# One reciprocal of eight columns in place of two of four, for the two head groups of a q tile

## Chip, cores and metric

The kernel runs on one core of one Trainium2 chip. The metric is the device time of one execution, in microseconds (us); several runs are taken and their median is quoted. The profile is of one further execution, recorded instruction by instruction.

## What is computed

Random-feature attention, followed by two feed-forward blocks, all in float32:

```
phi(x) = exp(x @ omega.T - |x|^2/2 - max) / sqrt(M)
kv  = einsum('bhsm,bhsd->bhmd', phi(k), v)
z   = sum over s of phi(k)
num = einsum('bhsm,bhmd->bhsd', phi(q), kv)
den = einsum('bhsm,bhm->bhs', phi(q), z) + 1e-06
x   = num / den                        # 4 batches x 8 heads x 576 x 64
x   = softplus(x @ w_in) @ w_out       # 2304 tokens, 512 -> 2048 -> 512
out = ((x @ w1) * (x @ w2)) @ w3 @ w_out2
```

## The kernel before

The 2304 tokens are 18 tiles of 128. A first stage makes `kv` for each batch and group of four heads, with `z` as a 65th column beside the 64 of `v` (a column of ones is appended to `v`). A second stage, the **q stage** (the loop at L767, from about 55 to 133 us of the span), turns the 18 q tiles into `x`. Then come the large products of the feed-forward blocks, from about 123 us to the end; they take some 680 of the 811 us.

In the q stage a tile is worked on in two **units**, one for each group of four heads. For a unit, in the order of the dataflow:

- `q_feat` (L393, with `project` at L339): twelve matmuls into one PSUM bank; `nmax`, the row maximum, by VectorE (L349, DVE in the profile); then four exponentials by ScalarE (L354, ACT) into `qp`.
- `q_turn` (L406): transposes of `qp` by TensorE (L409, PE) into a PSUM bank and one copy out by ACT (L411) into `qpt`.
- `q_num` (L413): the matmuls of `qpt` with `kv` (L96, recorded as `ps<-kv,qpt`) into a bank of their own, 65 columns for each head: 64 of the numerator and one of the denominator. Then three operations of DVE, each on four heads: L426 adds a small constant to the four denominators and writes them to a small tile `den`, L427 takes the reciprocal of these four columns in place, and L430 multiplies the 256 numerators by them and writes half of `xt`. L430 is the last reader of the bank.

After both units, `x_turn` (L435) transposes the tile's `xt` on PE (L439), ACT or DVE copies the result out (L444 or L442), and a DMA of the SP queue writes it to a DRAM tensor `xd`. When six tiles are there, `operands` (L448) reads them back for the first feed-forward product.

The stages are shifted against each other: in step t of the loop the features of tile t, the transposes of tile t-2, the numerators of tile t-3 and the `x_turn` of tile t-4 are issued. In odd steps `numerators` (L762) runs at the start and in even steps at the end, so that two tiles, four units, follow each other on PE with no other work between them. There are eight such pairs and two single tiles at the ends. The splitting of the weights and of the operands for the next stage is put into the same loop from a list, at fixed rates for each step.

All products of the kernel share eight PSUM banks (`ps`, L81), taken in turn. A new product waits until the last reader of the bank is done. The order of each engine's instructions is fixed when the program is built: a scheduler takes instructions in the order of the code but lets a later one pass an earlier one that it estimates is not ready yet. So DVE's order in the trace mixes units, and puts other work between two steps of a unit. Each engine runs its list strictly in that order.

The denominators of two consecutive units already lie in one tile of 2 x 4 columns (`pair`, L274, with three buffers).

Of the kernel before, what the change touches and what calls it, by code (L numbers as in the profile page):

```python
# [19 lines left out]
F32 = mybir.dt.float32  # L20
# [4 lines left out]
ALU = mybir.AluOpType  # L25
AX = mybir.AxisListType

B, H, S, D = 4, 8, 576, 64
M = 128
NT = B * S  # L30
# [41 lines left out]
def body(ctx: ExitStack, tc: tile.TileContext, q, k, k_rest, v, v_rest, om_t, w_in, w_out, w12, w3, wo, out):  # L72
    nc = tc.nc
    cp = ctx.enter_context(tc.tile_pool(name="cp", bufs=1))
    sm = ctx.enter_context(tc.tile_pool(name="sm", bufs=1))
    M_ = ctx.enter_context(tc.tile_pool(name="M_", bufs=14))
# [6 lines left out]
    def ps():  # L83
        return ps_.tile([128, 512], F32, tag="ps", name="ps")
# [10 lines left out]
    def matmul(o, a, b, start, stop, **kw):  # L95
        nc.tensor.matmul(out=o, lhsT=a, rhs=b, start=start, stop=stop, **kw)  # L96
# [177 lines left out]
    def pair(name, bufs):  # L274
        n = small.get(name, (None, 1))[1]
        if n:
            small[name] = sm.tile([128, 2, 4], F32, tag=name, bufs=bufs, name=name), 0
        else:
            small[name] = small[name][0], 1
        return small[name][0][:, 1 - bool(n)]  # L280
# [9 lines left out]
    kt, vt, kps, kpr, kvs, qts, kacc, raw = {}, {}, {}, {}, {}, {}, {}, {}  # L290
# [84 lines left out]
    def matmul_half(o, a, b, start, stop):  # L375
        for c in range(0, a.shape[-1], HALF):
            matmul(o[c:c + HALF], a[:, c:c + HALF], b, start, stop, skip_group_check=True)
# [11 lines left out]
        nc.scalar.copy(out=kvs[b][:, 4 * g:4 * g + 4, :], in_=acc)  # L389

    qp, qpt, xt = {}, {}, {}

    def q_feat(u):  # L393
        t, g = divmod(u, 2)
        p = project(lambda p: [x[:, 2 * g + p, :] for x in qts[t]])
        if g and t >= NT // 128 - len(EARLY):
            free["X0"] += 2

        def exps():
            qp[u] = M_.tile([128, 4, M], F32, tag="m", name="qp")  # L400
            features(*p, qp[u])

        waiting.append(exps)
        flush(QLAG)
# [5 lines left out]
        qpt[u] = M_.tile([128, 4, 128], F32, tag="m", name="qpt")  # L410
        nc.scalar.copy(out=qpt[u], in_=tp.rearrange("p (h t) -> p h t", h=4))  # L411

    def q_num(u):  # L413
        t, g = divmod(u, 2)
        nm = ps()
        nm = nm[:, 0:4 * (D + 1)].rearrange("p (h d) -> p h d", h=4)
        lo, hi = 128 * t, 128 * t + 128
        for h in range(4):
            a = lo
            while a < hi:  # L420
                b = a // S
                e = min(hi, (b + 1) * S)
                matmul_half(nm[a - lo:e - lo, h, :], qpt[u][:, h, a - lo:e - lo], kvs[b][:, 4 * g + h, :], True, True)
                a = e
        den = pair("den", 3)[:, :, None]
        nc.vector.tensor_scalar(out=den, in0=nm[:, :, D:D + 1], scalar1=1e-6 * M, scalar2=None, op0=ALU.add)  # L426
        nc.vector.reciprocal(out=den, in_=den)  # L427
        if g == 0:
            xt[t] = M_.tile([128, H, D], F32, tag="m", name="xt")
        nc.vector.tensor_tensor(  # L430
            out=xt[t][:, 4 * g:4 * g + 4, :], in0=nm[:, :, 0:D],
            in1=den.to_broadcast([128, 4, D]), op=ALU.mult,
        )

    def x_turn(t):  # L435
        tp = ps()
# [314 lines left out]
    nt = NT // 128  # L751
    begun = None

    def fill():
# [3 lines left out]
            x = Up1(0, 0, UP_RATES["Up1"][0])  # L758
            begun = x, x.begin_parts()
        next(begun[1], None)  # L760

    def numerators(t):  # L762
        if 0 <= t < nt:
            for g in range(2):
                q_num(2 * t + g)

    for t in range(nt + XLAG):  # L767
        if t % 2:
            numerators(t - NLAG)
        for g in range(2):  # L770
            if 0 <= t - TLAG < nt:
                q_turn(2 * (t - TLAG) + g)
        for g in range(2):
            if t < nt:
                q_feat(2 * t + g)
            else:
                flush(0)
            step(JOB_Q[0 in xo])
        for x in [nt - len(EARLY) + n for n, at in enumerate(EARLY) if at == t] + [t + 2] * (t + 2 < nt - len(EARLY)):
            split_q(x)  # L780
            load_q()
        if t == 1:
            kv_sum(2 * B - 1)
            kstack.close()
            pools["X0"] = ctx.enter_context(tc.tile_pool(name="X0", bufs=28, side="right", reuse_waits="tile"))
        if t >= XLAG:
            x_turn(t - XLAG)
            for c in range(2):
                if t - XLAG == 2 * N // 128 * (c + 1) - 1:
                    xo[c], ops = operands(c, xd, "X0")  # L790
                    queue += ops
        if not t % 2:
            numerators(t - NLAG)
        if t in FILL:
            fill()
# [426 lines left out]
```

## Time and profile before

| | us |
|---|---|
| median of 3 runs | 811.22 |
| lowest, highest | 810.95, 811.86 |
| profiled execution, its own time | 813.02 |
| profiled execution, span of its instructions | 810.9 |

The span is the time from the first to the last recorded instruction. An operation's duration in the trace is longer than the time for which it keeps its engine: the next one can start before the end of the one before. Where the cost of one more instruction is asked, the distance from its start to the next start is what counts. The ends of matmuls are modelled, so PE's busy share is not its use; the number of matmuls in a stretch tells more.

### The profile page before, as it was taken

The page shows a single profiled execution, that of the slowest core. Times are in us where ns is not written, and L with a number is a line of the kernel's source. Part 1 is how long each engine was busy: PE and PEld are TensorE (multiplying, and loading weights), DVE is VectorE, ACT ScalarE, POOL GpSimd, SP SyncE. Part 2 cuts the span into 40 slices and gives each one's busy share as a digit, 9 for nine tenths or more (in the row PEclk, how much of TensorE's full clock was granted, in tenths as well). Part 3 has the DMA queues.
Part 4 walks back from the last instruction along what each step waited for, and adds up shares of the span by engine and source line. Part 5 has one row for each costly group of instructions (what it writes and reads, how often), then busy time and mean ns, then how long its engine had stood idle before and what let it go on. Part 6 is the DMA issues. An engine that isn't in the chain of part 4 may idle for free.

```text
span 810.9 us, 14465 instructions
## 1 busy us (share of the span) xinstructions
PE 804.0 (99%) x5462; PEld 752.4 (93%) x5462; DVE 602.3 (74%) x1022; ACT 441.2 (54%) x859; POOL 26.5 (3%) x29
## 2 busy tenths in 40 slices
PE   9999999999999999999999999999999999999998
PEld 8999999999999998888888889999999998889998
DVE  6999999878765676754569633897988876888861
ACT  6999998557445676646456432424335123674330
POOL 3033300000000000000000000000000000000000
PEclk9999999999999999999999999999999999999999
DMA  9833635656535558688994642365656556353212
GB/s 288 327 100 87 201 107 172 210 205 214 195 133 195 191 193 259 214 258 293 335 304 148 208 127 79 133 217 186 209 174 214 188 180 237 111 170 122 73 65 78
DMA packets 75861, 150.04 MB, mean 185 GB/s; under 512 B 7184, under 2 KB 44688, under 8 KB 75792
## 3 DMA queue, kind: packets, MB, share of 16 engines
q1 hardware_dynamic: 64016, 101.55, 38.1%
q10 hardware_dynamic: 11776, 47.57, 17.4%
q8 instruction: 43, 0.70, 0.4%
q14 instruction: 26, 0.21, 0.1%
HBM read 98.24 MB, written 50.86 MB: 184 GB/s over the span
## 4 chain that ended last, share of the span: by engine, by line
PE 92%; DVE 4%; DMA 2%; issue 1%; ACT 0%; POOL 0%; ACTq 0%; POOLq 0%
PE ps L96 90%; DMA xq<-xd 1%; PE ps L409 1%; DVE nmax L349 1%; DVE xt L430 1%; DVE s L462 1%; PE ps L439 0%; DVE c L517 0%; DMA rawq<-in_q 0%; DVE u L517 0%; DVE xa22l L472 0%; DVE xa12l L472 0%; DVE qt L297 0%; DVE qtl L298 0%; DVE tlo L191 0%
## 5 line engine op out<-in xcount | busy, mean ns | idle before, releaser
L96 PE MATMUL ps<-dhi,lo 128*128 128x512 f32 x256 | 99.6, 389 | 0.0
L96 PE MATMUL ps<-dlo,hi 128*128 128x512 f32 x256 | 99.6, 389 | 0.0
L96 PE MATMUL ps<-dhi,hi 128*128 128x512 f32 x256 | 99.4, 389 | 0.0
L642 DVE TENSOR_TENSOR dlo<-dn,dhi 128x512 fp32r<-128x512 f32 x64 | 43.8, 689 | 39.1 <-ACT dhi L641 23.0
L517 DVE TENSOR_TENSOR c<-ps,u 128x384 f32<-128x384 f32 x144 | 71.5, 550 | 0.8
L517 DVE TENSOR_TENSOR u<-ps,p 128x384 f32<-128x384 f32 x48 | 26.7, 556 | 53.9 <-PE ps L96 52.3
L524 ACT COPY p<-ps 128x384 f32<-128x384 f32 x48 | 23.0, 480 | 75.8 <-PE ps L96 57.3
L641 ACT CAST dhi<-dn 128x512 fp32r<-128x512 f32 x64 | 39.4, 619 | 45.2 <-DVE dlo L642 25.7
L142 DVE SCALAR_TENSOR_TENSOR f<-raw,f 128x1024 int32<-128x1024 f32 (+2 forms) x43 | 45.5, 1058 | 20.3 <-ACT raw L139 18.8
L557 ACT ACTIVATE c<-c 128x384 f32<-128x384 f32 x72 | 35.1, 524 | 46.8 <-DVE c L517 43.0
L96 PEld LDWEIGHTS ps<-dlo,hi 128*128 128x128 f32 x256 | 48.1, 188 | 10.0
L96 PEld LDWEIGHTS ps<-dhi,hi 128*128 128x128 f32 x256 | 48.1, 188 | 10.0
L96 PEld LDWEIGHTS ps<-dhi,lo 128*128 128x128 f32 x256 | 48.1, 188 | 9.8
L138 ACT ACTIVATE f<-raw,bias 128x1024 f32<-128x1024 int16 (+2 forms) x43 | 46.3, 1084 | 18.9 <-DMA raw<-in_w 9.3
L349 DVE TENSOR_REDUCE nmax<-ps 128x4 f32<-128x512 f32 x72 | 47.0, 683 | 6.2 <-PE ps L96 6.0
L139 ACT ACTIVATE raw<-raw,bias 128x1024 f32<-128x1024 int16 (+2 forms) x43 | 46.3, 1082 | 0.6
L148 DVE SCALAR_TENSOR_TENSOR f<-raw,f 128x1024 int32<-128x1024 int32 (+2 forms) x43 | 45.0, 1046 | 0.6
L354 ACT ACTIVATE qp<-ps,nmax 128x128 f32<-128x128 f32 x144 | 42.2, 457 | 2.4 <-DVE nmax L349 2.4
L354 ACT ACTIVATE kp<-ps,nmax 128x128 f32<-128x128 f32 x128 | 35.5, 460 | 6.0 <-DVE nmax L349 5.9
L96 PE MATMUL ps<-xs1h,thi 128*128 128x384 f32 x96 | 32.4, 337 | 0.2 <-DVE c L517 0.2
L96 PE MATMUL ps<-xs2h,thi 128*128 128x384 f32 x96 | 32.3, 336 | 0.0
L96 PE MATMUL ps<-xs2h,tlo 128*128 128x384 f32 x96 | 32.2, 335 | 0.0
(257 smaller groups left out, 2339.4 us busy)
## 6 DMA issues: line engine op xcount, KB each, us to landing
dn<-gd SPq DMA_DIRECT2D x64, 256.0 KB, 4.0
raw<-in_w ACTq DMA_DIRECT2D x16, 1023.8 KB, 5.8
gd<-c SPq DMA_DIRECT2D x80, 192.0 KB, 2.7
pd<-c SPq DMA_DIRECT2D x48, 192.0 KB, 2.7
raw<-in_w_out ACTq DMA_DIRECT2D x10, 767.8 KB, 4.6
raw<-in_w_in ACTq DMA_DIRECT2D x6, 1023.8 KB, 5.1
rawq<-in_q SPq DMA_DIRECT2D x18, 256.0 KB, 3.1
xd<-xs SPq DMA_DIRECT2D x18, 256.0 KB, 3.3
```

What stands on the lines that cost most here:

```text
L96: nc.tensor.matmul(out=o, lhsT=a, rhs=b, start=start, stop=stop, **kw)
L138: nc.scalar.activation(out=self.f, in_=top, func=AF.Relu, scale=TOP, bias=bias[:, 0:1])
L139: nc.scalar.activation(out=self.words(1, F32, 2), in_=top, func=AF.Identity, scale=TOP, bias=bias[:, 1:2])
L142: nc.vector.scalar_tensor_tensor(out=self.f.bitcast(I32), in0=self.words(1, F32, 2), scalar=-2.0 ** 31, in1=self.f, op0=ALU.max, op1=ALU.min)
L148: nc.vector.scalar_tensor_tensor(out=fi, in0=self.words(0, I32, 2), scalar=13, in1=fi, op0=ALU.logical_shift_right, op1=ALU.bitwise_or,)
L349: nc.vector.tensor_reduce(out=nmax, in_=pj, axis=AX.X, op=ALU.max, negate=True)
L354: nc.scalar.activation(out=dst[:, h, :], in_=pj[:, h, :], func=AF.Exp, bias=nmax[:, h:h + 1])
L517: nc.vector.tensor_tensor(out=z, in0=bank, in1=y, op=ALU.add)
L524: nc.scalar.copy(out=p6, in_=b1)
L557: nc.scalar.activation(out=dst, in_=src, func=AF.Softplus)
L641: nc.scalar.copy(out=hi, in_=got[m])
L642: nc.vector.tensor_tensor(out=lo, in0=got.pop(m), in1=hi.bitcast(F32), op=ALU.subtract)
```

## The change

`q_num` for a unit and `numerators` for a tile become one function for a tile. It issues the matmuls of both units into two banks, then both additions into one tile `den` of 2 x 4 columns, then one reciprocal of the eight columns, then both multiplications. The matmuls, the additions and the multiplications are the same instructions as before, 36 of each of the two DVE operations; the reciprocals are 18 in place of 36. The `den` tile has the same size and number of buffers as before. The helper moves up in the file, and `nt` with it.

```diff
--- before.py
+++ after.py
@@ -389,6 +389,7 @@
         nc.scalar.copy(out=kvs[b][:, 4 * g:4 * g + 4, :], in_=acc)
 
     qp, qpt, xt = {}, {}, {}
+    nt = NT // 128
 
     def q_feat(u):
         t, g = divmod(u, 2)
@@ -410,27 +411,31 @@
         qpt[u] = M_.tile([128, 4, 128], F32, tag="m", name="qpt")
         nc.scalar.copy(out=qpt[u], in_=tp.rearrange("p (h t) -> p h t", h=4))
 
-    def q_num(u):
-        t, g = divmod(u, 2)
-        nm = ps()
-        nm = nm[:, 0:4 * (D + 1)].rearrange("p (h d) -> p h d", h=4)
+    def numerators(t):
+        if not 0 <= t < nt:
+            return
+        nms = []
         lo, hi = 128 * t, 128 * t + 128
-        for h in range(4):
-            a = lo
-            while a < hi:
-                b = a // S
-                e = min(hi, (b + 1) * S)
-                matmul_half(nm[a - lo:e - lo, h, :], qpt[u][:, h, a - lo:e - lo], kvs[b][:, 4 * g + h, :], True, True)
-                a = e
-        den = pair("den", 3)[:, :, None]
-        nc.vector.tensor_scalar(out=den, in0=nm[:, :, D:D + 1], scalar1=1e-6 * M, scalar2=None, op0=ALU.add)
+        for g in range(2):
+            nm = ps()[:, 0:4 * (D + 1)].rearrange("p (h d) -> p h d", h=4)
+            for h in range(4):
+                a = lo
+                while a < hi:
+                    b = a // S
+                    e = min(hi, (b + 1) * S)
+                    matmul_half(nm[a - lo:e - lo, h, :], qpt[2 * t + g][:, h, a - lo:e - lo], kvs[b][:, 4 * g + h, :], True, True)
+                    a = e
+            nms.append(nm)
+        den = sm.tile([128, 2, 4, 1], F32, tag="den", bufs=3, name="den")
+        for g in range(2):
+            nc.vector.tensor_scalar(out=den[:, g], in0=nms[g][:, :, D:D + 1], scalar1=1e-6 * M, scalar2=None, op0=ALU.add)
         nc.vector.reciprocal(out=den, in_=den)
-        if g == 0:
-            xt[t] = M_.tile([128, H, D], F32, tag="m", name="xt")
-        nc.vector.tensor_tensor(
-            out=xt[t][:, 4 * g:4 * g + 4, :], in0=nm[:, :, 0:D],
-            in1=den.to_broadcast([128, 4, D]), op=ALU.mult,
-        )
+        xt[t] = M_.tile([128, H, D], F32, tag="m", name="xt")
+        for g in range(2):
+            nc.vector.tensor_tensor(
+                out=xt[t][:, 4 * g:4 * g + 4, :], in0=nms[g][:, :, 0:D],
+                in1=den[:, g].to_broadcast([128, 4, D]), op=ALU.mult,
+            )
 
     def x_turn(t):
         tp = ps()
@@ -759,11 +764,6 @@
             begun = x, x.begin_parts()
         next(begun[1], None)
 
-    def numerators(t):
-        if 0 <= t < nt:
-            for g in range(2):
-                q_num(2 * t + g)
-
     for t in range(nt + XLAG):
         if t % 2:
             numerators(t - NLAG)
```

## Rows read from the trace of the kernel before

**Rows 1.** The page, part 1: busy time, share of the span and instructions of each engine.

```profile
PE 804.0 (99%) x5462; PEld 752.4 (93%) x5462; DVE 602.3 (74%) x1022; ACT 441.2 (54%) x859; POOL 26.5 (3%) x29
```

**Rows 2.** Stretches: length, busy us (x instructions) of PE, PEld, DVE, ACT, POOL, clock, DMA.

```profile
82.50:91.30 8.80, 8.02 (x113) 7.39 (x112) 8.74 (x24) 7.81 (x24) 3.29 (x3) 1.00 0.53 151
91.30:99.00 7.70, 7.70 (x116) 7.41 (x114) 7.02 (x20) 6.95 (x22) 3.06 (x3) 1.00 0.68 212
...
150.00:715.00 565.00, 565.00 (x2965) 524.73 (x2966) 401.24 (x648) 275.02 (x426) 0.00 (x0) 1.00 0.60 199
```

**Rows 3.** The waits of PE between 57 and 133 us: total, times, longest.

```profile
PE ps L409 <- ACT qp L354: 0.6, 2, 0.4
PE ps L96 <- ACT xs L444: 0.6, 1, 0.6
PE ps L96 <- DVE den L426: 0.4, 1, 0.4
PE ps L439 <- DVE den L427: 0.3, 1, 0.3
```

**Rows 4.** The chain of waits in order of time: start us, us, what.

```profile
69.29 0.03 DVE qth L297
...
86.01 0.42 DVE xt L430
...
86.58 1.67 PE ps L96 x12
...
149.89 565.66 PE ps L96 x2966
```

**Rows 5.** DVE by line and shape, 54 to 133 us: xcount, busy us, mean ns, idle before.

```profile
L349 DVE TENSOR_REDUCE nmax<-ps 128x4 f32<-128x512 f32 x35 | 23.1, 683 | 1.2 <-PE ps L96 1.1
...
L427 DVE RECIPROCAL den<-den 128x4 f32<-128x4 f32 x36 | 5.8, 168 | 0.1
...
L426 DVE TENSOR_SCALAR den<-ps 128x4 f32<-128x4 f32 x36 | 4.6, 141 | 0.0
```

**Rows 6.** DVE's timeline (start us, us, line, operation): one unit alone, then interleaved units.

```profile
92.60 0.15 DVE L426 TENSOR_SCALAR den<-ps 128x4 f32<-128x4 f32 x1
92.78 0.18 DVE L427 RECIPROCAL den<-den 128x4 f32<-128x4 f32 x1
93.07 0.43 DVE L430 TENSOR_TENSOR xt<-ps,den 128x256 f32<-128x256 f32 x1
...
94.15 0.17 DVE L427 RECIPROCAL den<-den 128x4 f32<-128x4 f32 x1
94.23 0.13 DVE L426 TENSOR_SCALAR den<-ps 128x4 f32<-128x4 f32 x1
```

**Rows 7.** DVE's timeline, the last unit of a group and what runs inside it.

```profile
110.86 0.17 DVE L427 RECIPROCAL den<-den 128x4 f32<-128x4 f32 x1
110.95 0.93 DVE L472 TENSOR_TENSOR xs1l<-s,xs1h 128x768 fp32r<-128x768 f32 x1
111.79 0.42 DVE L430 TENSOR_TENSOR xt<-ps,den 128x256 f32<-128x256 f32 x1
```

**Rows 8.** DVE's timeline, the first unit of the group that PE waits for.

```profile
85.07 0.15 DVE L426 TENSOR_SCALAR den<-ps 128x4 f32<-128x4 f32 x1
85.14 0.68 DVE L298 TENSOR_TENSOR qtl<-rawq,qth 128x512 fp32r<-128x512 f32 x1
85.74 0.17 DVE L427 RECIPROCAL den<-den 128x4 f32<-128x4 f32 x1
85.83 0.13 DVE L426 TENSOR_SCALAR den<-ps 128x4 f32<-128x4 f32 x1
86.01 0.42 DVE L430 TENSOR_TENSOR xt<-ps,den 128x256 f32<-128x256 f32 x1
```

**Rows 9.** PE's timeline around the same group, with the idle time before.

```profile
82.47 2.09 PE L96 MATMUL ps<-kv,qpt 128*64 128x65 f32 x64
...
86.58 0.36 PE L96 MATMUL ps<-omh,qt 128*128 128x256 f32 x1 [0.41 <-DVE den L426]
```


## Prediction

> **What bounds the kernel now.** I read the page's busy shares first. PE is busy for 99% of the span and DVE for 74% [rows 1]; a change that only takes work off DVE can pay only where DVE, for a while, is what PE waits for. So the next view is the table by stretches. From 150 to 715 us PE holds 565.00 of 565.00 us while DVE is busy for 401.24 [rows 2]: nothing that DVE saves is felt there, and none of the changed lines runs there. The chain of waits says the same: from 149.89 us it lies on PE for 565.66 us [rows 4]. What the change touches is the q stage, 55 to 133 us.
>
> In that stage the stretches show two kinds of pair of tiles. From 91.3 to 99.0 us a pair takes 7.70 us, PE busy throughout, DVE for 7.02. From 82.5 to 91.3 us a pair of about the same number of matmuls takes 8.80 us, and DVE is busy for 8.74 of them [rows 2]. So the stage runs at PE's pace of about 7.7 us for a pair and is held up at times, here by DVE. How much in all? The waits of PE in the stage are 0.6, 0.6, 0.4 and 0.3 us, 1.9 us together [rows 3]. That is the first bound: an edit of the q stage that removed every recorded wait would bring 1.9 us of 811, or 0.23%.
>
> The chain of waits shows where DVE counts. It is on DVE from 69.29 us to the multiplication at 86.01, with no other engine between, and then goes over to PE at 86.58 [rows 4]. That handover is seen on PE's timeline: after the 64 numerator matmuls from 82.47 and the transposes, PE stands still for 0.41 us before 86.58 [rows 9]. The view names a `den` addition as the releaser, but the one at 85.83 had ended by 85.96, 0.6 us earlier; what ends in time is the multiplication of the first unit, 86.01 + 0.42 = 86.43 [rows 8]. PE waited for that unit's bank.
>
> **What is removed.** Eighteen reciprocals of four columns. One has a duration of 168 ns [rows 5], but the next instruction starts after 94.23 - 94.15 = 0.08 us, or 85.83 - 85.74 = 0.09 us in the other place [rows 6, 8]. I take 0.085 us, so 18 x 0.085 = 1.53 us of DVE's time. Most of it lies under PE: in the pairs in which PE runs without a gap it is worth nothing, because the next matmul waits for no multiplication; if that cover were gone, the rest of it would count too. On the chain of DVE, 69.3 to 86.6 us, lie two whole groups of two tiles: 2 x 2 reciprocals fewer, **-0.34 us**. Bounds for this term: 0 and -1.53.
>
> The Trainium skill (Perfetto Trace Analysis, "Optimizing Scalar/DVE Operations") gives about 60 ns of access overhead for a DVE instruction on SBUF and advises grouping where the engine is saturated. By that figure the 18 would save 18 x 0.06 = 1.08 us as an estimate, against the 1.53 of the rows.
>
> **What is added: four columns to each remaining reciprocal.** The trace has no reciprocal of eight. From below: the maximum over 512 columns takes 683 ns and the addition on four takes 141 [rows 5], (683 - 141) / 508 = 1.07 ns a column, so 4 ns more. From above: all that the reciprocal takes beyond the addition, 168 - 141 = 27 ns, is put down to its four columns and paid again, with the 4: 31 ns. On the four reciprocals of the chain that is 0.02 to 0.12 us. I take **+0.02**, the value per column of a whole instruction being the nearer row.
>
> **What is moved: the order within a tile.** Each of three operations needs the one before it. A unit alone shows what this costs: addition to reciprocal 92.78 - 92.60 = 0.18 us, reciprocal to multiplication 93.07 - 92.78 = 0.29 us, where the engine could have started the next thing after 0.08 [rows 6]. Now units hide this for each other: between a reciprocal and its multiplication lies the addition of the next unit. In the new order, addition, addition, reciprocal, multiplication, multiplication, the second addition has its reciprocal right behind it, and the reciprocal its first multiplication. From above: each tile pays (0.18 - 0.08) + (0.29 - 0.08) = 0.31 us of idle time, 1.24 us for the four tiles on the chain. From below: nothing, where the next tile's additions or some other ready work stands between. In a group of two tiles the second tile's additions can cover the wait of the first reciprocal's reader, and the first tile's multiplications that of the second reciprocal. What has no cover within the group is the first reciprocal: 0.10 us in each of two groups, **+0.20 us**.
>
> **The wait that is made longer.** The first multiplication, which frees the first bank, now also stands behind the second unit's addition, so behind its matmuls. Sixty-four matmuls of four units take 2.09 us on PE [rows 9], so the second unit is ready 0.5 us after the first. In the group that PE waits for this is free: its matmuls began at 82.47, the second unit was complete by about 83.5, and DVE came to the first addition only at 85.07 [rows 8, 9]. Its order was addition, a subtraction of 0.60 us to the next start, reciprocal (85.74), addition, multiplication (86.01). In the new order the second addition stands at 85.74, the reciprocal 0.18 later at 85.92 and the multiplication 0.29 behind that at 86.21: PE goes on 0.20 us later, **+0.20 us**. Bounds: -0.09 (the multiplication moves up by the place of a short instruction) to +0.31 as above. Queued on DVE behind the longer wait are the next units' additions and the next maxima, for which ACT's exponentials wait; they too come 0.20 us later, but PE's twelve matmuls for the next maximum begin only after the freed bank, so they are not late twice.
>
> Buffers bring nothing either way: `den` has its three buffers as before, `xt` one tile per q tile, and no DMA is moved or added; SP, ACT and POOL issue what they did.
>
> **Sum.** -0.34 + 0.02 + 0.20 + 0.20 = +0.08 us, on the profiled execution's 813.02 us. That execution ran 1.80 us above the median of 811.22, so the forecast for the median is 811.22 + 0.08 = **811.3 us**. All ends together: -1.53 - 0.09 = -1.6 to 0.12 + 1.24 + 0.31 = +1.7 us, that is 809.6 to 813.0.
>
> **The rivals.** *Faster.* DVE's list gets short enough that PE never waits in the stage. For it: DVE is the engine that holds the slow pair, 8.74 of 8.80 us, and the slow pair is 8.80 - 7.70 = 1.10 us longer than the dense one [rows 2]; and in many groups the last unit's multiplication now stands behind a long piece of other work, as at 110.86, where a subtraction fills 0.84 us between the reciprocal and its reader at 111.79 [rows 7], a place that the new order fills with multiplications. Against it: 1.2 of the 1.9 us of PE's waits name ACT, not DVE [rows 3]. If all waits went: 811.2 - 1.9 = 809.3 us.
>
> *Slower.* The bank of the first unit is freed late. The mechanism is the scheduler's filling: the place behind the second addition and the place behind the reciprocal are open, and a subtraction of 0.84 us as in [rows 7] can be laid there, where now it comes behind the last unit's reciprocal. Then the first multiplication, and PE's next product, come later by that. It decides where PE is already short of a bank; I count the three largest of PE's waits, all at or above 0.4 us in total [rows 3], as such places. Price: 3 x 0.84 = 2.5 us, 813.7 us. For it: the subtraction of 0.68 us that stands between the first addition and its reciprocal at 85.14 [rows 8] shows that such places are filled. Against it: what fills them is work that had to be done anyway, and in dense pairs there is time. The Trainium skill's page named above also says that where Vector isn't saturated but makes other engines wait, splitting instructions can let work end sooner; merging is the reverse, and that rule points to this rival. Rows 8 and 9 agree that PE does wait for a multiplication.
>
> *It does not do what it says.* The eight-column reciprocal costs as much as two of four: then the saving of 0.34 us is gone, 811.6 us, which is within the forecast's own range.
>
> **How the numbers follow.** The measurement of this kernel can tell about 0.2%, 1.6 us, from no change. Forecast, with the third rival in it: 0.66, all within 0.2%. Faster rival: 0.16. Slower rival: 0.18, a little more since the terms that lengthen the path are surer than a gain on PE. The range for 8 in 10 takes the ends of the sum, 809.6 to 813.0, and a part of either rival: 809.3 to 813.4.
>
> **What would show it.** In the profile of the changed kernel: 18 reciprocals at L427's successor, with a mean of 172 to 199 ns and DVE's busy total lower by about 18 x 0.168 = 3 us; as many matmuls as before; the additions in twos ahead of each reciprocal; PE's waits between 57 and 133 us of 1.5 to 2.4 us in sum; the stretch from 150 us on as long as before. The sum is wrong where the slow pairs shrink to 7.7 us (then DVE's saving reached PE), or where new waits of PE for multiplications of 0.5 us and more appear behind the numerators (then a filler delays the bank), or where the stretches behind 150 us change at all, which no step here accounts for.

## The result and the profile after

The changed kernel takes 817.12 us (median of 6 runs, 816.64 to 817.82). The kernel before took 811.69 us in the same comparison (6 runs, 810.95 to 812.37). The ratio is **1.0068, 95% interval 1.0055 to 1.0081** (the ratios in this document are those on record, which can differ by 0.1 points, once by 0.2, from the quotient of two medians): slower by 5.4 us, where 811.3 was forecast, and outside the range up to 813.4. The sign is that of the rival called slower, 0.18 of the chances, and the time lies beyond its price too (813.7).

The profiled execution of the changed kernel took 817.09 us, with a span of 814.9. That of before took 813.02 with a span of 810.9, and lay 1.3 us above its median of this comparison. So the two traces differ by 4.0 us and not by 5.4; the traces account for the former.

The page of the changed kernel, part 1, against [rows 1] (busy us, share of the span, instructions):

```profile
PE 803.2 (99%) x5462; PEld 752.0 (92%) x5462; DVE 601.0 (74%) x1004; ACT 442.6 (54%) x859; POOL 26.5 (3%) x29
```

The edit did what it says: 18 instructions fewer on DVE, as many matmuls as before. DVE's busy time fell, and the kernel got slower. The operations themselves, DVE by line and shape, 54 to 140 us of the changed kernel (busy us, mean ns of one, idle before them), against [rows 5]:

```profile
L435 DVE TENSOR_TENSOR xt<-ps,den 128x256 f32<-128x256 f32 x36 | 13.5, 418 | 0.4
L431 DVE TENSOR_SCALAR den<-ps 128x4 f32<-128x4 f32 x36 | 4.8, 151 | 1.3 <-PE ps L96 1.1
L432 DVE RECIPROCAL den<-den 128x8 f32<-128x8 f32 x18 | 3.6, 199 | 0.2
```

A reciprocal of eight columns takes 199 ns where one of four took 168; the reciprocals went from 5.8 us to 3.6. Nothing here is as large as 4 us. So the place of the loss has to be found first. The stretches of the changed kernel (length, busy us and instructions of PE, PEld, DVE, ACT, POOL, clock, DMA), cut where the numerator matmuls of each pair of tiles begin:

```profile
75.40:84.60 9.20, 8.07 (x115) 7.45 (x114) 7.88 (x21) 7.56 (x25) 3.61 (x3) 1.00 0.59 168
...
92.60:100.20 7.60, 7.60 (x113) 7.40 (x112) 6.71 (x18) 7.11 (x22) 2.56 (x2) 1.00 0.77 220
100.20:110.70 10.50, 8.42 (x115) 7.44 (x114) 9.40 (x21) 8.51 (x25) 0.00 (x0) 1.00 0.39 119
...
150.00:719.00 569.00, 569.00 (x2993) 529.30 (x2992) 403.11 (x652) 276.49 (x426) 0.00 (x0) 1.00 0.59 198
```

The last row is to be read first: from 150 us on PE is busy for all of 569.00 us, as in [rows 2], at the same clock. Nothing is lost there. In the q stage the six stretches from one pair's burst to the next take 7.6 to 8.0 us in four cases, as the one from 92.60, which is PE's pace; one takes 9.20 and one 10.50, where the slowest pairs of before took 8.9 (8.80 in [rows 2], by its rounder ends). The stretch ahead of them, from the single first tile's burst to the first pair's, went from 6.70 us (60.10 to 66.80) to 7.21 (60.50 to 67.71). DVE is not busy throughout in either: 7.88 of 9.20 and 9.40 of 10.50. From the first burst of numerator matmuls to the last full one it is 55.5 us before (60.10 to 115.57) and 57.8 after (60.50 to 118.34), so 0.4 us of the 4.0 come ahead of the first burst, 2.4 between them and 1.2 behind them, where the last tile is.

The waits of PE in the stage, 54 to 140 us, changed kernel (total, times, longest), against [rows 3]:

```profile
PE ps L444 <- DVE xt L435: 1.6, 1, 1.6
PE ps L410 <- ACT qp L354: 1.6, 3, 0.7
PE ps L96 <- ACT xs L449: 0.8, 1, 0.8
PE ps L410 <- DVE xt L435: 0.8, 2, 0.6
PE ps L444 <- ACT qpt L412: 0.8, 1, 0.8
PE ps L410 <- ACT xs L449: 0.7, 1, 0.7
PE ps L96 <- DVE xt L435: 0.5, 1, 0.5
```

They come to 6.8 us, where those of before come to 1.9: 4.9 us more, with PE's busy time (whose ends are modelled) 0.8 us less. So the 4.0 us between the two spans are in this list. Three of the seven name the multiplication (L435), 2.9 us together. No row of [rows 3] does so by name; the prediction read the 0.4 us of `den` L426 as one. What DVE did ahead of these multiplications is in its timeline (start us, duration us, line and operation, count, and in brackets idle time before and its releaser). Three tiles of the changed kernel:

```profile
77.12 0.22 DVE L431 TENSOR_SCALAR den<-ps 128x4 f32<-128x4 f32 x2
77.31 0.20 DVE L432 RECIPROCAL den<-den 128x8 f32<-128x8 f32 x1
78.80 0.43 DVE L297 CAST qth<-rawq 128x512 fp32r<-128x512 f32 x1 [1.28 <-DMA rawq<-in_q]
79.14 0.42 DVE L435 TENSOR_TENSOR xt<-ps,den 128x256 f32<-128x256 f32 x1
...
101.78 0.22 DVE L431 TENSOR_SCALAR den<-ps 128x4 f32<-128x4 f32 x2
102.64 0.96 DVE L467 TENSOR_TENSOR s<-xq 128x768 f32<-128x768 f32 x1 [0.64 <-DMA xq<-xd]
103.51 0.20 DVE L432 RECIPROCAL den<-den 128x8 f32<-128x8 f32 x1
...
103.74 0.42 DVE L435 TENSOR_TENSOR xt<-ps,den 128x256 f32<-128x256 f32 x1
...
133.06 0.16 DVE L431 TENSOR_SCALAR den<-ps 128x4 f32<-128x4 f32 x1 [0.63 <-PE ps L96]
133.14 0.95 DVE L467 TENSOR_TENSOR s<-s,xq 128x768 f32<-128x768 f32 x1
134.01 0.16 DVE L431 TENSOR_SCALAR den<-ps 128x4 f32<-128x4 f32 x1
134.08 0.95 DVE L477 TENSOR_TENSOR xs1l<-s,xs1h 128x768 fp32r<-128x768 f32 x1
134.94 0.20 DVE L432 RECIPROCAL den<-den 128x8 f32<-128x8 f32 x1
135.06 0.91 DVE L477 TENSOR_TENSOR xs2l<-s,xs2h 128x768 fp32r<-128x768 f32 x1
135.88 0.75 DVE L435 TENSOR_TENSOR xt<-ps,den 128x256 f32<-128x256 f32 x2
```

In the first tile the reciprocal is done at 77.51, and its multiplication starts at 79.14, since a cast stands between that waits 1.28 us for a load. In the second a sum that waits 0.64 us for a load stands between the additions and the reciprocal. In the last tile every gap is filled by a piece of 0.9 us: 2.8 us from the first addition (133.06) to the first multiplication (135.88). What PE does then (its timeline, changed kernel):

```profile
79.70 0.36 PE L96 MATMUL ps<-omh,qt 128*128 128x256 f32 x1 [0.51 <-DVE xt L435]
...
136.35 0.44 PE L444 MATMUL ps<-ident,xt 128*128 128x128 f32 x2 [1.62 <-DVE xt L435]
```

After the first tile PE stands for its multiplication 0.51 us and, at 81.70, 0.62 for one of the next tile; after the last 1.62. After the second tile, waits of 0.82 and 0.68 us for copies of ACT follow, of which the kernel before has one too (0.55 us); that the late multiplication makes them is not shown.

A fourth place lies earlier. A subtraction of the weight splitting (`tlo`, L191) runs on DVE at 65.04 us, ahead of two maxima, where in the kernel before it ran at 71.21. It looks costly, but PE's only wait in that stretch, 0.68 us for exponentials, ends at 65.24, before these maxima run. What stands ahead of those exponentials is on ACT's list: the cast `thi` (L187), which `tlo` needs, in the changed kernel at 62.62 us, in the kernel before at 68.83. ACT's timeline and PE's wait, changed kernel, and last ACT's timeline of the kernel before:

```profile
62.62 1.32 ACT L187 CAST thi<-t 128x1024 fp32r<-128x1024 f32 x1
63.57 1.35 ACT L412 COPY qpt<-ps 128x512 f32<-128x512 f32 x2
64.52 2.49 ACT L354 ACTIVATE qp<-ps,nmax 128x128 f32<-128x128 f32 x8
...
65.24 0.33 PE L410 MATMUL ps<-ident,qp 128*128 128x128 f32 x1 [0.68 <-ACT qp L354]
...
68.83 1.15 ACT L187 CAST thi<-t 128x1024 fp32r<-128x1024 f32 x1
```

None of these fillers is new work. They were in the lists before, at other places. Of 1004 positions of DVE's list 219 differ between the two kernels, and in the others too: PE 127 of 4835, ACT about 160 of 938, SP some 20 of 369 (counted place by place, against the changed kernel's instructions put in the order of before; one piece that moves shifts all that it passes, so fewer pieces than that were moved). So the question for the runs: is it the shared reciprocal that costs, or the order that the scheduler made of it?

### The profile page after: what moved, and what is told of

It is laid out like the page before. It is cut to its first block, busy times and chain, and to the rows that moved or that the text cites. A ratio compares the mean times of both kernels' runs of the same rounds, so it can differ in the third digit from the quotient of the medians.

```text
span 814.9 us, 14450 instructions
## 1 busy us (share of the span) xinstructions
PE 803.2 (99%) x5462; PEld 752.0 (92%) x5462; DVE 601.0 (74%) x1004; ACT 442.6 (54%) x859; POOL 26.5 (3%) x29
## 4 chain that ended last, share of the span: by engine, by line
PE 87%; ACT 6%; DVE 3%; DMA 2%; issue 1%; SPq 0%; POOL 0%; DVEq 0%; ACTq 0%; POOLq 0%
PE ps L96 86%; ACT qp L354 2%; ACT kp L354 2%; ACT qpt L412 1%; DMA xq<-xd 1%; DVE nmax L349 1%; DVE xt L435 1%; PE ps L410 0%; PE ps L444 0%; DMA rawq<-in_q 0%; DMA xd<-xs 0%; ACT xs L449 0%; ACT f L138 0%; ACT raw L139 0%; ACT thi L187 0%
## 5 line engine op out<-in xcount | busy, mean ns | idle before, releaser
L96 PE MATMUL ps<-xs3h,thi 128*128 128x384 f32 x96 | 32.2, 335 | 0.0
```

## The experiments

All comparisons are with the kernel before on the same chip (medians of 811.69 to 812.69 us). Where a quoted expectation names a theory by a letter, the text behind it says how it fared. In the labels, **old order** and **new order** are the issue lists of the kernel before and of the changed kernel; **own** means two reciprocals of four columns, **shared** one of eight. The lists were tied by the same few lines at the end of the body, which chain each engine's instructions by an order edge and add no wait (shortened; `...` marks what is left out, and a pair stands for a place in the program's own order and a count):

```diff
+    issue_in(tc, ORDER)
...
+ORDER = {
+    mybir.EngineType.PE: [(0, 1207), (1209, 1), (1207, 2), ...
...
+def issue_in(tc, order):
...
+    for engine, runs in order.items():
+        seq = [traced[engine][a + n] for a, c in runs for n in range(c)]
+        for x, y in zip(seq, seq[1:]):
+            tc.add_manual_dep(y, x.name, behind, reason="issue order")
```

### Order and reciprocal, taken apart

**old_order_own** is the control: the kernel before with all its lists tied to what they are anyway.

> The kernel before, with every instruction of PE, DVE, ACT and SP tied behind the one that it follows there today: the same lists, now written down. A control of the method. All theories: within 0.2% of the kernel before, about 811 to 812 us.

Measured: 812.51 us, ratio 1.0004 (0.9995 to 1.0013). Tying costs nothing that can be measured.

**old_order_shared** is the changed kernel's arithmetic in the order of before; each shared reciprocal stands where the second of the two stood, the first multiplications behind it.

> The changed kernel's instructions in the order of the kernel before: PE, ACT and SP exactly as there, on DVE the shared reciprocal at the place of the second unit's reciprocal and the first unit's multiplication moved right behind it. Theory A (the loss comes from the order in which the scheduler laid out all engines anew, not from the shared reciprocal): 811 us within 1 us, ratio to the kernel before 0.998 to 1.002. Rival B (the loss is the shared reciprocal's own: both units must be complete before the first multiplication, and both banks are held longer): 814 to 817 us. Rival C (an eight-column reciprocal is slow): its duration would be near twice 168 ns, and the time above 812 us.

Measured: 814.86 us, 1.0025 (1.0015 to 1.0036). The larger part of the loss is gone, not all: theory A's 0.998 to 1.002 is missed, and the time lies at the lower end of rival B's range. C fails: the trace has 0.20 us for a reciprocal.

**new_order_own** is the other crossing: the arithmetic of before in the order of the changed kernel, with the two reciprocals one behind the other at the place of the shared one.

> The kernel before, two four-column reciprocals for a tile, in the order of the changed kernel: PE, ACT and SP exactly as there, on DVE both reciprocals back to back at the place of the shared one. Theory A (order): 816 to 818 us, as the changed kernel, or a little more for 18 short instructions. Rivals B and C (the shared reciprocal itself): 811 to 813 us for C; B expects 814 to 817 here too only in so far as both reciprocals now stand behind the second unit's addition.

Measured: 817.64 us, 1.0065 (1.0051 to 1.0078), as slow as the changed kernel with its 1.0068. Its waits of PE, 54 to 140 us (total, times, longest):

```profile
PE ps L439 <- DVE xt L430: 1.7, 1, 1.7
PE ps L409 <- ACT qp L354: 1.6, 3, 0.7
PE ps L96 <- ACT xs L444: 0.9, 1, 0.9
PE ps L439 <- ACT qpt L411: 0.9, 1, 0.9
PE ps L96 <- DVE xt L430: 0.8, 1, 0.8
PE ps L409 <- ACT xs L444: 0.7, 1, 0.7
PE ps L409 <- DVE xt L430: 0.7, 1, 0.7
```

Row for row this is nearly the list of the changed kernel (the code and the line numbers are those of before). Theory A's range holds. **The order alone, without a shared reciprocal, costs what the change costs.** The four together:

| | two of four (own) | one of eight (shared) |
|---|---|---|
| old order | 1.0004 | 1.0025 |
| new order | 1.0065 | 1.0068 (the changed kernel, not tied) |

The order costs 0.6 points with two reciprocals and 0.4 with one; sharing costs 0.2 points in the old order (0.21, with an uncertainty of 0.14) and nothing that can be told from zero in the new.

**two_recips_joint** lets the scheduler lay out the same joint form again (both additions, then two reciprocals of four, then both multiplications), with nothing tied.

```diff
-        nc.vector.reciprocal(out=den, in_=den)
+        for g in range(2):
+            nc.vector.reciprocal(out=den[:, g], in_=den[:, g])
```

> The changed kernel's function with two four-column reciprocals (both additions, both reciprocals, both multiplications), laid out by the scheduler. Theory A: the time goes by what order the scheduler makes of it, anywhere from 810 to 818 us, and no nearer to the changed kernel than its lists are. Rivals B and C: as the additions stand in twos here too, B expects 815 to 817 us; C expects 811 to 812 us, as no reciprocal is wide.

Measured: 813.69 us, 1.0022 (1.0013 to 1.0031). Theory A left this open; B and C fail. One more instruction for each tile, and the scheduler arrives at a layout that loses a third as much. The joint form does not have to lose 5 us.

### Which part of the order

**new_order_no_fill**: the changed kernel's lists, but on DVE the five instructions of each tile stand together, at the place of the second addition.

> The changed kernel's own lists on PE, ACT and SP; on DVE the five instructions of each tile (two additions, reciprocal, two multiplications) stand together at the place of the second addition, and whatever the scheduler had put between them comes behind. Theory D (what the scheduler filled in between additions, reciprocal and multiplications costs the time: pieces of 0.4 to 1.9 us, some of which wait for a DMA): 812.5 to 814.5 us, PE's waits for xt gone. Rival E (the lists of PE and ACT, and work pulled ahead, cost it; the fill only moves the waits): 816 to 818 us.

Measured: 816.82 us, 1.0058 (1.0045 to 1.0072). The theory that the fillers within a tile are the cause fails as it was put. The waits of PE, 54 to 140 us, show why:

```profile
PE ps L410 <- ACT qp L354: 4.3, 6, 1.6
PE ps L96 <- ACT qpt L412: 1.3, 1, 1.3
PE ps L410 <- DVE xt L435: 0.4, 1, 0.4
```

Waits for multiplications are down from 2.9 to 0.4 us, and waits for ACT's exponentials up from 1.6 to 4.3. The fill, maxima among it, now comes behind the five instructions, and the exponentials need the maxima: ACT's own waits for maxima go from 1.7 to 2.6 us. So what one tile gains the work behind it on the same list pays. Rival E's range holds.

**new_order_late_loads** moves only the two pieces that stand for a load behind the multiplication or the additions that they blocked.

> The changed kernel's own lists, but on DVE two pieces of fill that stood still for a DMA are moved: the cast qth that waited 1.3 us at 78.8 us (with its subtraction) behind the next tile's multiplications, and the sum s that waited 0.6 us at 102.6 us behind the next additions. Theory D1 (half of the loss or more is DVE standing still for loads in the middle of a tile's five instructions): 815 to 816 us. Rival: the waits move on to ACT or to the next load: 817 us.

Measured: 816.22 us, 1.0050 (1.0036 to 1.0064), between the two forecasts; that half of the loss or more lies here is not borne out. **new_order_tail** puts only the last tile's five instructions together.

> The changed kernel's own lists, but on DVE the five instructions of the last tile stand together and the three sums and subtractions that lay between them (2.6 us) come behind. Theory D2 (PE's last two waits before the transposes of the last tile, 0.8 and 1.6 us, are lost time): 815.3 to 816 us. Rival (PE has the first feed-forward product to fill the wait, or is late for it anyway): 817 us.

Measured: 816.33 us, 1.0053 (1.0037 to 1.0068). This too lies between its forecasts. The intervals of both overlap that of the changed kernel; each gain, 0.15 to 0.18 points, is of the size of the uncertainty.

**new_order_three** does both, and moves `tlo` back to where it stood in the kernel before.

> The changed kernel's own lists on PE, ACT and SP; on DVE four places are mended: the two pieces that waited for loads, the last tile's five instructions together, and the 1.2 us subtraction tlo, which the new list has 3 us earlier ahead of two maxima, back behind the reciprocal of tile 2. Theory M (the loss is the sum of these places on DVE): the first two brought 1.2 and 1.0 us, tlo stands before 0.5 us of the first group's 7.2 us: 814 to 815 us. Rival: the waits move on, 816 us or more.

Measured: 815.51 us, 1.0041 (1.0026 to 1.0055). The time lies between theory M and its rival. Four places bring 0.27 of the 0.68 points, less than half, with an uncertainty of 0.2. The waits that name multiplications are gone but for 0.4 us; what is left is again mostly the exponentials:

```profile
PE ps L410 <- ACT qp L354: 2.5, 5, 0.7
PE ps L444 <- ACT qpt L412: 0.8, 1, 0.8
PE ps L410 <- ACT xs L449: 0.7, 1, 0.7
PE ps L410 <- DVE xt L435: 0.4, 1, 0.4
```

Moving `tlo` shows no gain in this trace. The first stretch still takes 7.2 us (60.65 to 67.86) with PE's wait of 0.68 in it, and the two maxima start at 66.89 us where they started at 66.94: DVE now stands idle for 1.61 us ahead of them, until PE's products for them are there. So `tlo` had filled a pause, and the expectation's 0.5 us for it fails.

### Which engine's list

In these three the changed kernel has one engine tied to the order of before, and the scheduler lays out the rest. **new_pe_old** ties PE's list.

> The changed kernel with only PE's list tied to that of the kernel before; the scheduler lays out the others, and DVE's, ACT's and SP's lists stay nearer to the changed kernel's than to the kernel before's. Theory H (the new PE list, with transposes of one unit put between the matmuls of the next, makes PE wait for ACT's exponentials): 814 to 815.5 us, that is, no more than the old order with the shared reciprocal. Rival I (DVE's and ACT's lists carry the loss): 816 to 818 us.

Measured: 818.30 us, 1.0090 (1.0060 to 1.0121): no gain, and theory H fails. One of the four runs, 824.94 us, widens the interval; the other three lie between 817.97 and 818.56. **new_act_old** ties ACT's.

> The changed kernel with only ACT's list tied to that of the kernel before; the scheduler lays out the others, PE's list stays the changed kernel's in most of its differences, DVE's comes out between the two. Theory J (ACT's list, in which work for the next stage was pulled ahead of exponentials and copies, carries the loss): 813 to 815 us. Rival H (PE's list): 816 to 818 us.

Measured: 817.10 us, 1.0057 (1.0039 to 1.0074): no gain that can be told from none, and theory J fails. The stretch that `thi` had lengthened is back at 6.7 us (61.05 to 67.75), but PE's waits for multiplications are 4.2 us in place of 2.9. The expectation has PE's list wrong: in this program it differs from that of before at 50 positions and from the changed kernel's at 127, so the loss stays with ACT's list and most of PE's as before, and 118 positions of DVE's still different. **new_dve_old** ties DVE's.

> The changed kernel with only DVE's list tied to the old order (shared reciprocal at the place of the second unit's); the scheduler lays out PE, ACT and SP, and comes within 12, 5 and 2 places of the kernel before's lists. Theory L (DVE's list is what carries the loss; the other lists follow from it): 813 to 815 us, as the old order with all lists tied. Rival (PE's and ACT's few remaining differences cost it): 816 us or more.

Measured: 815.10 us, 1.0029 (1.0017 to 1.0042), where old_order_shared with all lists tied had 1.0025. With DVE's list as before, the scheduler's own choices for PE, ACT and SP come out within 12, 5 and 2 places of before's. Theory L's range is missed by 0.1 us, its rival's by more. **Tying DVE's list alone removes more than half of the loss**, as much as tying all; the other lists follow it. What is not shown is how much of the loss lies on DVE itself: DVE's old list was not run under the new lists of PE and ACT, where `thi` is a place of its own.

### What the shared reciprocal costs in the old order

old_order_shared is 0.25% slower than the kernel before. DVE's timeline of it shows one place that the sum has no term for:

```profile
93.79 0.20 DVE L432 RECIPROCAL den<-den 128x8 f32<-128x8 f32 x1
94.47 0.42 DVE L435 TENSOR_TENSOR xt<-ps,den 128x256 f32<-128x256 f32 x1 [0.48 <-DVE den L432]
...
100.62 0.96 DVE L467 TENSOR_TENSOR s<-xq 128x768 f32<-128x768 f32 x1 [1.91 <-DMA xq<-xd]
```

The multiplication starts 0.68 us after its reciprocal, and the engine stands still for 0.48 us after the reciprocal's end at 93.99. PE waits 0.81 us for that multiplication. Later DVE stands 1.91 us for a load of `x`, and ACT 2.20. The standstill is seen at the same multiplication in new_dve_old (0.49 us). The multiplication waits for its reciprocal and for a copy of ACT into `qpt`, and both were done by 94.00 us. Two theories: the late load is what costs, or the standstill and the longer chain are.

**old_order_shared_late** moves the pieces that wait for that load further back on DVE and ACT.

> The shared reciprocal in the order of the kernel before, with the first use of the loads xq (three sums, two subtractions on DVE, two casts on ACT) some 3 to 8 us later in the lists. In the run without this the 2.4 us over the kernel before were lost between 91.6 and 110.6 us, where DVE waited 1.9 us and ACT 2.2 us for xq. Theory F (the shared chain makes x a few tenths later, the load that needs it comes later still, and both in-order engines stand still for it with the q stage's work behind): 811 to 813 us. Rival G (the time is lost to the first multiplication that comes late, PE waiting 0.8 us for it and its consequences): 814 to 815 us.

Measured: 814.38 us, 1.0030 (1.0020 to 1.0039): no gain. Theory F fails, G's range holds: the late load is not the cost. **old_order_own_late** moves the same pieces in the kernel before, an attempt to beat both.

> The kernel before in its own order, with the first use of the loads xq (three sums, two subtractions on DVE, two casts on ACT) some 3 to 8 us later in the lists: a try for a kernel that beats both. DVE stood still 0.3 us and ACT 0.6 us for them, and PE 0.9 us behind that: 811 to 812 us, 0.5 to 1 us under the kernel before, if nothing later waits for the operands; no change if PE's waits move on.

Measured: 813.47 us, 1.0015 (1.0005 to 1.0025): a miss. PE waits 0.7 us for a copy of DVE (`xs`) instead.

**old_order_shared_pad** puts 24 tiny writes ahead of everything on DVE, which shifts the position of all its later instructions in DVE's program and nothing else in their order.

```diff
     bias = cp.tile([128, 2], F32, name="bias")
+    for _ in range(24):
+        nc.vector.memset(bias[:, 0:1], 0.0)
```

> The shared reciprocal in the order of the kernel before, with 24 small writes of a constant more at the start of DVE's list, so that every later DVE instruction lies 24 places further in its program. In both runs of this order DVE stood still for 0.48 us between the reciprocal and the first multiplication of tile 7. If that is a load of DVE's code, the standstill moves to another instruction, and the time falls to 812 to 813.5 us where it no longer lies ahead of a multiplication that PE waits for. If it is GpSimd, whose operation ended 0.05 us before it both times, it stays at tile 7 and the time at 814 to 815.5 us.

Measured: 813.84 us, 1.0015 (1.0001 to 1.0029), between the two ranges, with single runs from 812.14 to 816.77. The gain of 0.10 points on the order without padding has an uncertainty of 0.17, so the time shows none. The trace shows the standstill gone. The same tile, DVE's timeline:

```profile
93.70 0.20 DVE L434 RECIPROCAL den<-den 128x8 f32<-128x8 f32 x1
94.01 0.42 DVE L437 TENSOR_TENSOR xt<-ps,den 128x256 f32<-128x256 f32 x1
```

From the reciprocal to the multiplication it is now 0.31 us instead of 0.68, though GpSimd runs the same operation at the same time (its timeline, padded kernel), so GpSimd was not what held it:

```profile
93.07 1.27 POOL L300 TENSOR_TENSOR qt<-rawq,qt 128x512 fp32r<-128x512 f32 x1 [0.42 <-DVE qt L299]
```

PE's wait behind it went from 0.81 to 0.43 us. A standstill that goes away when instructions ahead of it in the list are added fits a load of DVE's program from memory that fell between these two. The traces hold packets of 8192 bytes on a queue that they call instruction. In the three kernels with the standstill one of them starts 0.66 to 0.68 us after the start of the late multiplication (at 95.13 us in old_order_shared); in the padded kernel one starts at 84.23 and the next not before 99.58. So such packets do go with this place in the list, and move with the padding. But this one comes after the standstill and cannot be what the multiplication waited for, so the cause stays inferred.

Two controls. **old_order_own_pad** pads the kernel before:

> The kernel before in its own order with the 24 small writes: what the padding does by itself. Theory: within 0.2% of the kernel before, 811.5 to 813.5 us. If it comes out 1 us or more faster, the padded runs are to be compared with this one, and the shared reciprocal in the old order is dearer than the padded run says.

Measured: 812.88 us, 1.0005 (0.9996 to 1.0015): as the kernel before. **new_order_pad** pads the changed kernel in its own order, where the rival was that such standstills make the loss:

> The changed kernel in its own lists with the same 24 small writes ahead on DVE. In the old order they moved a load of DVE's code off a tile's five instructions and brought about 1 us. Theory A (the loss is the order): 816 to 818 us, as the changed kernel. Rival K (the loss is where DVE's code loads happen to fall): 812 to 814.5 us.

Measured: 817.33 us, 1.0059 (1.0044 to 1.0074). Theory A's range holds and that rival fails: the loss of the changed kernel is not of this kind. This run is also the control for tying the new order: its lists are the changed kernel's own. That the writes moved a load of code and brought about 1 us is said more firmly in the expectation than the runs show, as above.

No version beat the kernel before.

## Why the prediction was wrong

**What held.** The stretch from 150 us on is unchanged, as many matmuls run, the reciprocals are 18 with a mean of 199 ns, the upper bound (31 ns more than 168). The saving is as small as it was said to be: in the last tile the next start comes 135.06 - 134.94 = 0.12 us after a shared reciprocal, against 2 x 0.085 for two, so 0.05 us for each tile and 0.9 us over 18, nearly all under other work. The sum itself was worked for the order of before, and the runs in that order lie within its bounds or at their upper end. Against its control, sharing costs 0.21 points (1.0025 and 1.0004), some 1.7 us with an uncertainty of 1.1; padded, 0.10 points (1.0015 and 1.0005), some 0.8 us with one of 1.4. The sum had +0.08 and an upper end of +1.7. The eight-column reciprocal alone was under-sized: its next start came 0.035 us later than that of one of four (0.12 and 0.085), just above the upper of the two bounds (0.031) where 0.005 was taken. (811.22 + 1.67 is 812.9, not 813.0; nothing hangs on it.)

**The step that failed** is "What is moved: the order within a tile". The prediction kept DVE's list as the trace of before shows it and re-sorted only the five instructions of a tile ("From below: nothing, where the next tile's additions or some other ready work stands between"). The same holds for "SP, ACT and POOL issue what they did": the same work, but not in the same order. The list is made anew by the scheduler, for all engines, and the change of order got no term. About one position in five of DVE's list is different. new_order_own shows that the new order alone costs 0.65%, some 5 us, with no reciprocal shared; old_order_shared and its padded form show that without it 0.15 to 0.25% is left. The prediction's own sign of this error is in the trace: waits of PE for multiplications of 0.51, 0.62 and 1.62 us, and 6.8 us of waits where 1.5 to 2.4 were expected.

**The slower rival came nearest, and is not the whole cause.** It named the scheduler's filling, and put three places at 0.84 us. Filled places are what the trace shows, with more than the filler's length: two of the fillers wait for a load, on an engine that runs in order, so that 1.28 and 0.64 us of waiting are added to the pieces' own time; and at the last tile, which the rival did not count because PE's wait there was the smallest of the four (0.3 us), PE stands for 1.62 us. But new_order_no_fill takes the filling away in every tile and is hardly faster (1.0058): the waits move to ACT's exponentials. The prediction named that path ("Queued on DVE behind the longer wait are the next units' additions and the next maxima, for which ACT's exponentials wait") and priced it at nothing. And work that is pulled forward on ACT, such as `thi`, delays exponentials too, which no term had.

The forecast for DVE's busy time was off too: 1.3 us less, not 3. The reciprocals gave 2.2, and `tlo` took back 0.77 (below).

The Trainium skill (Perfetto Trace Analysis, "Optimizing Scalar/DVE Operations") has the rule that splitting can finish work sooner where an engine makes others wait; the prediction put it beside the slower rival. The sign of the result agrees. But splitting the reciprocal alone, in the new order and still behind both additions, gains nothing (new_order_own), so most of the time was not lost by this mechanism; the 0.1 to 0.2 points that sharing costs in the old order may be.

**The account.** Of 0.68 points, by the ratios: the step from the changed kernel to new_order_three, four places on DVE of which `tlo` shows no gain, 0.27; from there to old_order_shared, the rest of DVE's order and the lists of PE, ACT and SP, 0.16; padding, 0.10; what then is left against the kernel before, 0.15, of which 0.05 is seen in the control as well. Each of these differences has an uncertainty of about 0.1 to 0.2 points. Only the first, and that the order costs more than the sharing, are clear of it; how much goes to sharing depends on the order in which it is measured, as the table shows.

**Open.** Which places make the 0.16 points is not settled: the waits that are left name exponentials five times, at most 0.7 us each. Why the scheduler lays other things into the places of a shared reciprocal, and finds a better layout with two reciprocals than with one, was not traced into its estimates. `thi` was not moved back by itself. A version with the shared reciprocal, tied by hand and tuned, was not tried beyond these.

## What to carry to other kernels

In a program whose order is laid out by a scheduler, an edit that changes what waits for what changes every engine's list; compare the issue orders of the two kernels before pricing instructions, and tie the old order under the new arithmetic to separate the edit from the layout. Merging short instructions saves here some 0.05 us for a pair, while one piece that waits for a DMA, laid into the chain that frees a PSUM bank, kept DVE idle for 0.6 to 1.3 us. Read a gap on an in-order engine by what stands ahead of the late instruction, not by the engine's busy time: it fell by 1.3 us and the kernel's time rose. And before a piece that moved is blamed, look at whether anyone waited behind it: `tlo` stood ahead of two maxima that could hardly have run earlier.

## What the runs showed of the hardware

A pause of DVE of 0.48 us with nothing visible to wait for, at the same instruction in three kernels and gone with 24 more instructions ahead in the list, as shown above. What it costs is not told from the noise.

A subtraction with both inputs in SBUF stretched from 1.20 to 1.97 us beside an operation of GpSimd. In the changed kernel, DVE's timeline:

```profile
65.04 1.97 DVE L191 TENSOR_TENSOR tlo<-t,thi 128x1024 fp32r<-128x1024 f32 x1
```

and GpSimd's:

```profile
64.66 1.28 POOL L298 TENSOR_TENSOR qt<-rawq,qt 128x512 fp32r<-128x512 f32 x1 [0.95 <-PE ps L410]
```

In the kernel before the same subtraction starts at 71.21 us, with GpSimd idle from 70 to 73, and takes 1.20. GpSimd's operation ends at 65.94, and 65.94 + 1.20 = 67.14 is close to the subtraction's end at 67.01: it looks as if it had started after GpSimd. In new_order_own the same overlap gives the same 1.97 us, and in new_order_three, moved to 71.31 with GpSimd idle, it takes 1.17. The Trainium skill (SBUF — State Buffer, "SBUF: two separate sides") says that the two engines share a pair of ports under an exclusive lock, for DVE operations with two SBUF inputs too, and that the later one waits for the whole instruction; the row agrees. The multiplication at 94.01 above, whose numerators lie in PSUM, took its usual 0.42 us beside GpSimd. So an order that moves a piece under a GpSimd operation also changes the piece's own length.
